# GpSimd's first expert subtractions cut in halves and tied to the routing rounds' comparisons; sixteen filler matmuls a round in place of fifteen

## The chip, the core and the metric

The kernel runs on one core of one Trainium2 chip. Its engines work in parallel, each through a queue of its own: TensorE (PE in the profile, PEld for its weight loads), VectorE (DVE), ScalarE (ACT), GpSimd (POOL) and SyncE (SP), which only issues DMAs here. The metric is the device time of one execution in microseconds, lower is better.

## The reference, cut to what matters

Attention with a decay, a gated FFN, and a routed layer of eight experts follow each other:

```python
attn_out = _attn_ref(**attn_kwargs)                      # 4 x 8 heads, 576 tokens, 64
x = attn_out.transpose(0, 2, 1, 3).reshape(B * S, H * D)  # 2304 x 512
gate = 1.0 / (1.0 + np.exp(-(x @ w_gate)))
x = gate * (x @ w_val) @ w_out
logits = x @ w_gate2                                     # 2304 tokens, 8 experts
for idx in np.argsort(-logits.flatten()):                # best pairs first
    tok, e = divmod(idx, 8)
    if assigned[tok] < 0 and counts[e] < 288:
        assigned[tok] = e
        counts[e] += 1
for e in range(8):
    out[assigned == e] = np.maximum(x[assigned == e] @ w1[e], 0.0) @ w2[e]
```

## The kernel before

Float32 products are made of three matmuls: each operand is split into a high part (a rounded copy, made by ScalarE) and a low part (the operand less the copy, made by GpSimd or VectorE), and high-high, low-high and high-low are summed.

The program runs through attention, FFN, routing and experts. Routing is the place of the change. It needs the logits of all tokens; the FFN's last output matmuls (tokens of the last rows, 7 passes of 36 matmuls, L666, `Ffn.defer`) are kept back and handed out one at a time by `filler(n)`, so that TensorE has work while VectorE does the routing. Each pass ends with an eviction by ScalarE (L669) and a store of x2d by SyncE (L513). After the routing, `filler(1000)` runs what is left; then the experts start with a gather of their tokens from x2d by the indices `idx` (L979, on GpSimd's queue).

Routing is a search by rounds (`ROUNDS = 7`, numbered 0 to 6 here). In a round VectorE

- removes what fell below the last bounds (L786 reads the bounds in PSUM and the logits in SBUF; L787 reads two tiles in SBUF), chooses each token's best expert (L789, L791),
- subtracts the expert's bound (L798, L800, L802) and compares with 64 thresholds: L803, the long comparison, writes the tile `c` (shown as mr),

then TensorE counts in 18 small matmuls (L806) and gets `FILL[4] = 2` fillers, VectorE makes the next step from the counts (L809), TensorE adds it to the bounds in PSUM (L779) and gets `FILL[5] = 15` fillers (6 in the last round). All engines work in the order in which the program is written (a manual schedule), with a wait where one needs what another makes.

Beside this the first expert's first four weight blocks are made ready (`Experts`, blocks 0 to 3, each 128x1024): loaded by SyncE into one of two buffers `fraw`, copied to `ehi` by ScalarE (L956), subtracted to `elo` by GpSimd (L958). Before, `split(r)` stands behind each of rounds 0 to 3, with nothing that ties it to VectorE's place in the round; block n + 2 is loaded when block n is through. The other 60 blocks are split in the expert stage.

Of the kernel before, what the change touches and what calls it, by code (L numbers as in the profile page):

```python
# [6 lines left out]
F32 = mybir.dt.float32  # L7
F32R = mybir.dt.float32r
# [4 lines left out]
AF = mybir.ActivationFunctionType  # L13
OP = mybir.AluOpType
# [10 lines left out]
E = 8  # L25
# [335 lines left out]
class Weights:  # L361
# [5 lines left out]
    def __init__(self, ev, stage, w64):  # L367
        self.ev, self.stage, self.w64 = ev, stage, w64
        self.more, self.ahead = None, 2
        self.hi, self.lo, self.raw, self.b = [None] * NF, [None] * NF, {}, {}  # L370
# [43 lines left out]
class XLoader:  # L414
# [34 lines left out]
    def split(self, c, k, nk=1, steps=(0, 1, 2)):  # L449
        nc = self.ev.nc  # L450
        xh, xl = self.hi[c][:, k:k + nk], self.lo[c][:, k:k + nk]
        x = self.r[c, k]
        for step in steps:
            if step == 0:
                nc.vector.tensor_tensor(x, xl.bitcast(F32), x, op=OP.mult)
            elif step == 1:
                nc.scalar.activation(xh, x, AF.Copy)
            else:
                nc.gpsimd.tensor_tensor(xl, x, xh, op=OP.subtract)
                del self.r[c, k]  # L460


class Ffn:
# [180 lines left out]
    def logits(self, buf, fill):  # L644
# [4 lines left out]
        nc.vector.tensor_copy(s[:, TC:], self.lg[1][:16, :256])  # L649
        fill(FILL[0])  # L650
        p = self.bank()
# [21 lines left out]


TH = 64
FILL = (3, 5, 12, 10, 2, 15, 13, 18)
ROUNDS = 7
MORE = 24

# [22 lines left out]
class Route:  # L702
# [35 lines left out]
    def start(self, L):  # L738
# [6 lines left out]
        nc.vector.tensor_copy(self.Lm, L)  # L745
        self.fill(FILL[1])
        p = self.psum()
# [9 lines left out]
        nc.vector.tensor_scalar(up, s[:E], -1.0, None, op0=OP.mult)  # L757
        self.fill(FILL[2])
        self.lo = self.psum("o0")
        self.raise_by(up, True)  # L760
        self.fill(FILL[3])

# [28 lines left out]
        nc.vector.tensor_tensor(a, self.Lm, self.bcast_t(m), op=OP.is_equal)  # L791
        return a, m

    def round(self, first=False, fill=FILL[5]):
        nc, wk = self.nc, self.work
        a, m = self.choose(first)
        la = self.la
        nc.vector.tensor_tensor(la, a, self.bcast_e(self.lo[:, :E]), op=OP.mult)  # L798
        lt = wk.tile([128, NT], F32, name="r_lt")
        nc.vector.tensor_reduce(lt, la.rearrange("p e t -> p t e"), op=OP.add, axis=AX.X)  # L800
        u = wk.tile([128, NT], BF16, name="r_u")
        nc.vector.tensor_tensor(u, m, lt, op=OP.subtract)  # L802
        nc.vector.tensor_tensor(self.c, self.pairs(u, TH), self.row(self.gs), op=OP.is_ge)  # L803
        cnt = self.psum()
        for t in range(NT):
            nc.tensor.matmul(cnt[:E, :TH], a[:, :, t], self.c[:, t // 2, :, t % 2], start=t == 0, stop=t == NT - 1)  # L806
        self.fill(FILL[4])
        up = wk.tile([E, 1], F32, name="r_up", bufs=2)
        nc.vector.scalar_tensor_tensor(self.g, cnt[:E, :TH], CAP - 0.5, self.ds, op0=OP.is_ge, op1=OP.mult, accum_out=up)  # L809
        self.raise_by(up)  # L810
        self.fill(fill)
# [114 lines left out]
class Experts:  # L926
# [4 lines left out]
    def __init__(self, ev, first, w1, w2):  # L931
        self.ev, self.first, self.pool, self.w1, self.w2 = ev, first, None, w1, w2
        self.raw, self.hi, self.lo = {}, {}, {}

    def load(self, n, queue=None):
        queue = queue or self.ev.nc.sync
# [10 lines left out]
                queue.dma_start(r.rearrange("p (k d) -> p k d", k=2),  # L947
                                          self.w2[e, i * 256:(i + 1) * 256, :].rearrange("(k p) d -> p k d", p=128))

    def split(self, n):  # L950
        if n < 8 * E:
            nc, r = self.ev.nc, self.raw.pop(n)
            pool = self.first if n % 12 < 4 else self.pool
            hi = self.hi[n] = pool.tile([128, 1024], F32R, name=f"ehi{n % 12}", bufs=1)
            lo = self.lo[n] = pool.tile([128, 1024], F32R, name=f"elo{n % 12}", bufs=1)
            nc.scalar.activation(hi, r, AF.Copy)  # L956
            eng = nc.vector if n % 4 == 3 and n > 3 else nc.gpsimd
            eng.tensor_tensor(lo, r, hi, op=OP.subtract)  # L958
            if n < 2:
                self.load(n + 2)  # L960
            elif n > 3:
                self.load(n + RAWS)


RAWS = 4
# [122 lines left out]
def network(tc, qk, vv, f, ww, bcT, w1, w2, cb, cf, out):  # L1088
    nc = tc.nc
    ev = Env()  # L1090
    ev.nc, ev.tc = nc, tc
    with ExitStack() as ctx:
        ctx.enter_context(tc.manual_schedule())

        def pool(name, stack=ctx, side="left", bufs=1, **kw):
            return stack.enter_context(tc.tile_pool(name=name, bufs=bufs, side=side, reuse_waits="tile", **kw))

        ev.consts = pool("consts")
        dr = ctx.enter_context(tc.tile_pool(name="dram", bufs=1, space=bass.MemoryType.DRAM))
        xs = dr.tile([NHEAD, D + 1, S], F32, name="xs")  # L1100
        rec = dr.tile([NHEAD, S], F32, name="rec")
        ckd = dr.tile([2, NHEAD, S], F32, name="ckd")
        x2d = dr.tile([N, DM], F32, name="x2d")
        L = ev.consts.tile([128, E, NT], F32, name="L")
        ev.idx = ev.consts.tile([TT, 24], I32, name="idx")

        body, right = ExitStack(), ExitStack()
        xp = pool("xp", right, "right")
        w0, mix = pool("w0", body), pool("mix", body)
        W = Weights(ev, mix, ww)  # L1110
        W.tiles(w0, 0, -(-EARLY // 3))
        X = XLoader(ev, xp, xs, rec)
        xa = X.tiles(xp, "xa")
        X.put(0, xa)
        X.put(2, xa)
        X.put(4, xa)

        def fill(h):
            if h == -3:
                W.load(0)  # L1120
                W.load(1)
            elif h == -2:
                for step in range(3):
                    W.bits(0, step)
            elif h == -1:
                W.cut(0)
            count = lambda h: 3 + (h - 3) * (EARLY - 1) * 3 // 27
            jobs = lambda h: range(count(h), count(h + 1))
            for lag, do in enumerate((W.bits, lambda n, s: s == 2 and W.cut(n, (0,)),
                                      lambda n, s: s == 2 and W.cut(n, (1,)))):  # L1130
                if 3 <= h - lag < 30:
                    for i in jobs(h - lag):
                        do(*divmod(i, 3))
            if XF <= h < XF + 16:
                k, i = divmod(h - XF, 4)
                if i == 0:
                    X.load(0, k)
                else:
                    X.split(0, k, steps=(i - 1,))

        attention(ev, qk, vv, f, xs, rec, ckd, fill)

        W.tiles(pool("w1", body), -(-EARLY // 3), NF)
        work, ps = ExitStack(), ExitStack()
        xq = pool("xq", right, "right")
        W.more, W.ahead = xq, 4
        xb = X.tiles(xq, "xb")
        X.put(1, xb)
        X.put(3, xb)
        F = Ffn(ev, W, X, EARLY, bcT, x2d, L, pool("pg", ps, bufs=4, space=PSUM), pool("po", ps, space=PSUM))  # L1150
        F.wk, F.mix, F.right = pool("fw", work), mix, xq
        F.wp = F.wk.tile([128, NF, E], F32, name="wp")
        F.wpr = F.wk.tile([128, NF, 2 * E], F32R, name="wpr")
        F.regular()
        F.group()
        right.close()
        work.close()

        ep = pool("ep", side="right")
        tail = ExitStack()  # L1160
        rp, rw = pool("rp", tail), pool("rw", tail, bufs=2)
        scratch = [mix.tile([128, n], F32, name=m, bufs=1) for m, n in (("mr0", 1024), ("mr1", 1024), ("mb0", 512), ("mb1", 512))]
        xd, scratch[0] = scratch[0][:, :DM], scratch[0][:, DM:]
        EW = Experts(ev, ep, w1, w2)
        rest = F.defer(xd)

        def filler(n):
            for _ in range(n):
                if next(rest, 0) == 0:
                    break  # L1170

        R = Route(ev, rp, rw, F.bank, cb, cf, scratch, filler)
        EW.load(0)
        EW.load(1)
        F.logits(scratch[1], filler)
        R.start(L)
        for r in range(ROUNDS):
            R.round(r == 0, FILL[5] if r < ROUNDS - 1 else 6)
            if r < 4:
                EW.split(r)  # L1180
        a = R.settle()
        R.permutation(a)
        filler(1000)
        tail.close()
        body.close()
        ps.close()
        EW.pool = pool("ew")
        xw = pool("xw", bufs=2)
        pools = {n: pool("xp_" + n, bufs=b, space=PSUM) for n, b in (("h", 3), ("y", 2), ("t", 3))}
        experts(ev, EW, x2d, ev.idx, out, xw, lambda n: pools[n].tile([128, 512], F32, name="e" + n))  # L1190
# [30 lines left out]
```

## Time and profile before

| what | value |
|---|---|
| time, median of 3 runs | 943.69 us (939.49, 943.69, 945.07) |
| the profiled execution | 940.77 us, its span 939.1 us |
| granted TensorE clock, mean | 0.978 |
| busy: TensorE | 913.0 us, 97% of the span |
| busy: VectorE | 552.4 us, 59% |
| busy: GpSimd | 454.8 us, 48% |
| busy: ScalarE | 331.0 us, 35% |

All times within the execution count from the start of the span. Busy time of TensorE is pipelined matmuls, so that 97% busy does not mean 97% at full rate. A granted clock of 1.00 is 2.4 GHz, of 0.5 is 1.2 GHz; between the two stands a stretch that had both. A row of a timeline gives start, duration, engine, line, operation, output<-inputs with shapes, and in brackets how long the engine had stood idle and who ended that.

### The profile page before, as it was taken

To read this page: it belongs to the slowest core of one execution; us is meant where nothing else is said; L and a number is where in the kernel's file an instruction comes from. 1 tells how busy PE (TensorE), PEld (TensorE's weight loads), DVE (VectorE), ACT (ScalarE), POOL (GpSimd) and SP (SyncE) were. 2 spreads that over 40 slices of the span, in tenths; PEclk is the share of its full clock that TensorE was granted. 3 is DMA by queue.
4 is the path that set the end of the run, shared out by engine and by line. 5 is a ranking of instruction groups with operands and counts; after the bars stand their busy time and mean duration, and the time that the engine had idled before them with its cause. 6 is when DMAs were issued, how large, how long until landed. Compare 5 with 4: busy or idle time off the path is not lost. (4 is left out here: it accounts for less than half of the span.)

```text
span 939.1 us, 14062 instructions
## 1 busy us (share of the span) xinstructions
PE 913.0 (97%) x5188; PEld 767.1 (82%) x5188; DVE 552.4 (59%) x1188; ACT 331.0 (35%) x570; POOL 454.8 (48%) x376
## 2 busy tenths in 40 slices
PE   8899999999999999999999999998989999999996
PEld 4677777778788888888888888876779999999995
DVE  6467867737886387988989533536504434434431
ACT  4466667643232211121111222121016444444430
POOL 5678879843665122221222222124027787777741
PEclk7799999999999999999999999999899999999998
DMA  5687899754552202010111210012028666665610
GB/s 129 160 215 209 211 220 240 197 157 150 174 162 80 73 0 90 18 63 11 56 51 26 65 45 1 1 55 68 24 66 268 216 190 182 199 187 193 201 48 26
DMA packets 48873, 111.04 MB, mean 118 GB/s; under 512 B 11331, under 2 KB 11747, under 8 KB 48803
## 3 DMA queue, kind: packets, MB, share of 16 engines
q1 hardware_dynamic: 44642, 98.59, 36.6%
q0 software_dynamic: 3072, 9.44, 3.1%
q10 hardware_dynamic: 1088, 2.10, 0.7%
q8 instruction: 41, 0.67, 0.3%
q14 instruction: 30, 0.24, 0.1%
HBM read 86.12 MB, written 14.45 MB: 107 GB/s over the span
## 5 line engine op out<-in xcount | busy, mean ns | idle before, releaser
L497 POOL TENSOR_TENSOR gl<-sg,gh 128x512 fp32r<-128x512 f32 x36 | 50.0, 1388 | 200.9 <-ACT gh L496 200.9
L958 POOL TENSOR_TENSOR elo<-eraw,ehi 128x1024 fp32r<-128x1024 f32 x45 | 108.3, 2416 | 42.0 <-ACT ehi L956 41.6
L145 PE MATMUL pv<-e,vf 128*65 128x256 f32 (+1 forms) x434 | 106.3, 370 | 0.0
L490 PE MATMUL gv<-xah,w_hi 128*128 128x512 f32 (+1 forms) x288 | 103.2, 358 | 0.0
L490 PE MATMUL gv<-xal,w_hi 128*128 128x512 f32 (+1 forms) x288 | 102.9, 357 | 0.0
L490 PE MATMUL gv<-xah,w_lo 128*128 128x512 f32 (+1 forms) x288 | 102.8, 357 | 0.0
L530 DVE CUSTOM_DVE_ANT_0 mb<-mb,bc 128x512 f32<-128x512 f32 x96 | 82.2, 856 | 3.3
L530 DVE CUSTOM_DVE_ANT_0 mb<-mr,bc 128x512 f32<-128x512 f32 x96 | 82.4, 858 | 2.8
L1003 PE MATMUL eh<-xeh,ehi 128*128 128x288 f32 x256 | 78.3, 306 | 0.9 <-DVE hl L1006 0.9
L1016 PE MATMUL ey<-hh,ehi 128*128 128x288 f32 x256 | 78.0, 305 | 0.0
L496 ACT ACTIVATE gh<-sg 128x512 fp32r<-128x512 f32 x36 | 22.8, 633 | 156.5 <-PE o L509 84.3
L1003 PE MATMUL eh<-xel,ehi 128*128 128x288 f32 x256 | 76.7, 299 | 0.0
L1003 PE MATMUL eh<-xeh,elo 128*128 128x288 f32 x256 | 76.4, 299 | 0.0
L1016 PE MATMUL ey<-hl,ehi 128*128 128x288 f32 x256 | 76.4, 299 | 0.0
L490 PE MATMUL gv<-xbh,w_hi 128*128 128x512 f32 x192 | 76.1, 396 | 0.0
L490 PE MATMUL gv<-xbl,w_hi 128*128 128x512 f32 x192 | 76.1, 396 | 0.0
L490 PE MATMUL gv<-xbh,w_lo 128*128 128x512 f32 x192 | 76.0, 396 | 0.0
L1016 PE MATMUL ey<-hh,elo 128*128 128x288 f32 x256 | 75.7, 296 | 0.0
L169 DVE CUSTOM_DVE_ANT_0 mj<-p1b,mq 128x192 bf16<-128x192 f32 (+3 forms) x128 | 46.8, 419 | 45.6 <-PE p1b L145 45.6
L145 PE MATMUL p1b<-P 66*128 66x192 f32 (+7 forms) x256 | 69.3, 339 | 3.4 <-DVE mx L169 2.0
L145 PEld LDWEIGHTS pv<-e,vf 128*65 128x65 f32 x434 | 50.5, 139 | 24.1 <-issue 15.5
L1006 DVE SCALAR_TENSOR_TENSOR hl<-eh,hh 128x288 fp32r<-128x288 f32 x64 | 29.1, 456 | 61.5 <-ACT hh L1005 61.5
(202 smaller groups left out, 2289.1 us busy)
## 6 DMA issues: line engine op xcount, KB each, us to landing
eraw<-w SPq DMA_DIRECT2D x56, 512.0 KB
mr<-ww SPq DMA_DIRECT2D x26, 512.0 KB
raw<-qk SPq DMA_DIRECT2D x16, 576.0 KB
p<-P SPq DMA_DIRECT2D x64, 144.0 KB
vf<-vv SPq DMA_DIRECT2D x16, 330.0 KB
bc<-ww SPq DMA_DIRECT2D x10, 512.0 KB
xs<-xo SPq DMA_DIRECT2D x16, 292.5 KB
xr<-rec SPq DMA_DIRECT2D x32, 128.0 KB
```

The source lines that it names most:

```text
L145: nc.tensor.matmul(out, lhsT, rhs, start=start, stop=stop, skip_group_check=True)
L169: nc.vector.tensor_tensor_reduce(out=junk[:, JT[t]:JT[t] + n], in0=src, in1=ev.mq[:, S - n:], op0=OP.add, op1=OP.min, scale=-1.0, scalar=3 ...
L490: nc.tensor.matmul(p[i][:, :m], w_[:, ws], x_[:, k], start=n == 0, stop=n == 11)
L496: nc.scalar.activation(hi, s, AF.Copy)
L497: nc.gpsimd.tensor_tensor(lo, s, hi, op=OP.subtract)
L530: nc.vector.tensor_tensor_reduce(out=junk, in0=a, in1=self.bc[j], op0=OP.mult, op1=OP.add, scale=1.0, scalar=0.0, accum_out=res)
L958: eng.tensor_tensor(lo, r, hi, op=OP.subtract)
L1003: nc.tensor.matmul(p[:, :CH], w_[:, ws], x_[:, k], start=n == 0, stop=n == 11)
L1006: nc.vector.scalar_tensor_tensor(h[1][:, f], p[:, :CH], 0.0, h[0][:, f], op0=OP.max, op1=OP.subtract)
L1016: nc.tensor.matmul(p[:, :CH], w_[:, ws], h_[:, f], start=n == 0, stop=n == 23)
```

## The change

Blocks 0 to 2 are split in halves: in round r (1 to 6), right behind L803, half (r - 1) % 2 of block (r - 1) // 2. Ahead of each half GpSimd copies one element of `c` to a tile `gate`, which makes it wait for that round's L803. Block 3 follows in two halves behind `idx`. The whole block is still copied to ehi in one piece, with the first half. The next load is issued with the second half. And `FILL[5]` goes from 15 to 16.

```diff
-FILL = (3, 5, 12, 10, 2, 15, 13, 18)
+FILL = (3, 5, 12, 10, 2, 16, 13, 18)
...
-    def round(self, first=False, fill=FILL[5]):
+    def round(self, first=False, fill=FILL[5], beside=lambda: None):
...
         nc.vector.tensor_tensor(self.c, self.pairs(u, TH), self.row(self.gs), op=OP.is_ge)
+        beside()
         cnt = self.psum()
...
+        self.gate = first.tile([1, 1], F32, name="gate", bufs=1)
...
-    def split(self, n):
-        if n < 8 * E:
+    def split(self, n, part=None, after=None):
+
+        if part is not None:
+            nc, c = self.ev.nc, slice(512 * part, 512 * part + 512)
+            if part == 0:
+                self.hi[n] = self.first.tile([128, 1024], F32R, name=f"ehi{n % 12}", bufs=1)
+                self.lo[n] = self.first.tile([128, 1024], F32R, name=f"elo{n % 12}", bufs=1)
+                nc.scalar.activation(self.hi[n], self.raw[n], AF.Copy)
+            nc.gpsimd.tensor_copy(self.gate, after)
+            nc.gpsimd.tensor_tensor(self.lo[n][:, c], self.raw[n][:, c], self.hi[n][:, c], op=OP.subtract)
+            if part:
+                del self.raw[n]
+                if n < 2:
+                    self.load(n + 2)
+        elif n < 8 * E:
...
-            if n < 2:
-                self.load(n + 2)
-            elif n > 3:
-                self.load(n + RAWS)
+            self.load(n + RAWS)
...
         for r in range(ROUNDS):
-            R.round(r == 0, FILL[5] if r < ROUNDS - 1 else 6)
-            if r < 4:
-                EW.split(r)
+            R.round(r == 0, FILL[5] if r < ROUNDS - 1 else 6, lambda: r and EW.split((r - 1) // 2, (r - 1) % 2, R.c[:1, 0, :1, 0]))
         a = R.settle()
         R.permutation(a)
+        for part in range(2):
+            EW.split(3, part, ev.idx[:1, :1])
         filler(1000)
```

GpSimd's queue in the routing rounds, as a piece of the difference (- before, + after; mr_5456 is the tile c, and in brackets stand the semaphores waited for):

```order
 L497 TENSOR_TENSOR w_lo_2236<-mb_5398,w_hi_2235 128x256 [waits Activation_49]
-L958 TENSOR_TENSOR elo_5584<-fraw,ehi_5583 128x1024 [waits DMAHW1_49,DMAHW6_49,Activation_49,Pool_49]
-L958 TENSOR_TENSOR elo_5641<-fraw,ehi_5640 128x1024 [waits DMAHW2_49,PE_49,DMAHW7_49,Activation_49,Pool_49]
-L958 TENSOR_TENSOR elo_5702<-fraw,ehi_5701 128x1024 [waits DMAHW2_49,Activation_49]
-L958 TENSOR_TENSOR elo_5757<-fraw,ehi_5756 128x1024 [waits DMAHW3_49,Activation_49]
-L848 TENSOR_LOAD r_n [waits DVE_49]
-L850 COMPARE_AND_BRANCH
+L960 CAST gate<-mr_5456 1x1 [waits DVE_49,Activation_49,Pool_49]
+L961 TENSOR_TENSOR elo_5598<-fraw,ehi_5597 128x512 [waits DMAHW6_49,DMAHW1_49,Activation_49]
+L960 CAST gate<-mr_5456 1x1 [waits DVE_49]
+L961 TENSOR_TENSOR elo_5598<-fraw,ehi_5597 128x512
```

Before, four whole subtractions stand there that wait for ScalarE and the loads; after, each half has a gate that waits for VectorE in front of it (two more pairs of gates and halves follow, for blocks 1 and 2).

GpSimd's queue behind the routing, in the changed kernel (idx is the list of slots; L991 is the first expert's gather, L979 before):

```order
L851 UNCONDITIONAL_BRANCH [waits Pool_sequencer_49]
L960 CAST gate<-idx 1x1 [waits DVE_49,Pool_49]
L961 TENSOR_TENSOR elo_6140<-fraw,ehi_6139 128x512 [waits DMAHW5_49,Activation_49]
L960 CAST gate<-idx 1x1 [waits Pool_49]
L961 TENSOR_TENSOR elo_6140<-fraw,ehi_6139 128x512
L991 DMA xg<-x2d,idx 96x512 [waits DMAHW4_49,DMAHW3_49,DMAHW6_49,DMAHW1_49,DMAHW7_49,DMAHW0_49,PE_49]
```

Block 3 stands between the branch and the gathers now; before, the gathers followed the branch directly.

SyncE's queue in the rounds, as a piece of the difference (fraw<-w are the loads of blocks 2 and 3, x2d<-mr the stores of finished output rows):

```order
-L944 DMA fraw<-w 128x1024 [waits DMAHW6_49,DMAHW2_49,Pool_49]
-L944 DMA fraw<-w 128x1024 [waits DMAHW7_49,DMAHW3_49,Pool_49]
-L513 DMA x2d<-mr_5455 64x512 [waits DMAHW4_49,Activation_49]
-L513 DMA x2d<-mr_5455 64x512 [waits DMAHW5_49]
+L946 DMA fraw<-w 128x1024 [waits DMAHW2_49,DMAHW6_49,Activation_49,Pool_49]
+L513 DMA x2d<-mr_5455 64x512 [waits DMAHW3_49,Activation_49]
+L513 DMA x2d<-mr_5455 64x512 [waits DMAHW4_49]
+L946 DMA fraw<-w 128x1024 [waits DMAHW5_49,DMAHW7_49,Activation_49,Pool_49]
```

The load of block 3 has moved behind the second pair of stores.

## Rows read from the trace of the kernel before

**Rows 1.** Chain of waits, 610 to 712 us: start, duration, what.

```profile
680.50 10.78 PE o L666 x81
```

**Rows 2.** TensorE's waits in the span: us in total, times, longest.

```profile
PE gv L806 <- DVE mr L803: 3.7, 2, 1.9
```

**Rows 3.** Windows, L806 to L806: length; PE, PEld, DVE, ACT, POOL busy; clock; DMA.

```profile
630.17:635.44 5.27, 5.27 (x39) 3.91 (x38) 3.21 (x10) 2.41 (x3) 0.73 (x1) 1.00 0.10 24
635.44:642.51 7.07, 5.33 (x39) 3.91 (x38) 5.27 (x10) 0.08 (x1) 4.29 (x2) 1.00 0.56 162
642.51:647.77 5.26, 5.26 (x37) 3.91 (x38) 3.20 (x10) 1.90 (x3) 0.28 (x1) 1.00 0.05 18
647.77:655.02 7.25, 5.33 (x39) 4.00 (x39) 5.45 (x10) 0.59 (x1) 4.46 (x2) 1.00 0.14 33
655.02:663.28 8.26, 8.26 (x38) 6.04 (x37) 3.18 (x10) 0.60 (x1) 0.00 (x0) 0.59 0.06 21
```

**Rows 4.** VectorE's timeline, 634 to 681 us.

```profile
634.37 0.76 DVE L803 TENSOR_TENSOR mr<-r_u,r_cb 128x1152 bf16<-128x1152 bf16 x1
...
637.16 0.30 DVE L786 TENSOR_TENSOR mr<-r_lm,o 128x144 f32<-128x144 f32 x1 [0.76 <-PE o L779]
637.50 2.40 DVE L787 SCALAR_TENSOR_TENSOR r_lm<-mr,r_lm 128x144 f32<-128x144 f32 x1
...
641.70 0.76 DVE L803 TENSOR_TENSOR mr<-r_u,r_cb 128x1152 bf16<-128x1152 bf16 x1
...
644.57 0.31 DVE L787 SCALAR_TENSOR_TENSOR r_lm<-mr,r_lm 128x144 f32<-128x144 f32 x1
...
646.70 0.76 DVE L803 TENSOR_TENSOR mr<-r_u,r_cb 128x1152 bf16<-128x1152 bf16 x1
...
649.83 2.57 DVE L787 SCALAR_TENSOR_TENSOR r_lm<-mr,r_lm 128x144 f32<-128x144 f32 x1
...
680.75 0.18 DVE L922 SCALAR_TENSOR_TENSOR idx<-gv,r_pr 96x24 int32<-96x24 f32 x1
```

**Rows 5.** GpSimd's timeline, 630 to 700 us.

```profile
634.71 5.02 POOL L958 TENSOR_TENSOR elo<-fraw,ehi 128x1024 fp32r<-128x1024 f32 x2 [13.98 <-ACT ehi L956]
647.49 4.74 POOL L958 TENSOR_TENSOR elo<-fraw,ehi 128x1024 fp32r<-128x1024 f32 x2 [7.76 <-ACT ehi L956]
695.75 1.11 POOL L979 DMA_INDIRECT xg<-x2d,idx  x1 [43.52 <-issue]
697.16 0.92 POOL L979 DMA_INDIRECT xg<-x2d,idx  x1 [0.31 <-issue]
```

**Rows 6.** TensorE's timeline, 640 to 659 us.

```profile
640.15 0.39 PE L666 MATMUL o<-w_lo,w_hi 128*128 128x512 f32 x1
640.38 0.39 PE L666 MATMUL o<-w_hi 128*128 128x512 f32 x1
642.51 0.71 PE L806 MATMUL gv<-mr,r_a 128*8 128x64 bf16 x18 [1.74 <-DVE mr L803]
...
655.02 0.90 PE L806 MATMUL gv<-mr,r_a 128*8 128x64 bf16 x18 [1.92 <-DVE mr L803]
...
658.54 0.63 PE L666 MATMUL o<-w_hi 128*128 128x512 f32 x1
658.97 0.63 PE L666 MATMUL o<-w_hi,w_lo 128*128 128x512 f32 x1
```

**Rows 7.** GpSimd's groups by line and shape: count, busy us, mean ns, idle before.

```profile
L411 POOL TENSOR_TENSOR w_lo<-mb,w_hi 128x512 fp32r<-128x512 f32 x36 | 53.8, 1503 | 5.1 <-ACT w_hi L408 5.1
...
L203 POOL TENSOR_SCALAR_AFFINE_SELECT e<-e 128x256 f32<-128x256 f32 x32 | 13.9, 434 | 2.2
...
L497 POOL TENSOR_TENSOR w_lo<-gh,w_hi 128x512 fp32r<-128x512 f32 x4 | 5.2, 1292 | 20.8 <-ACT w_hi L496 20.8
...
L1034 POOL MEMSET gap<- 1x1 f32 x24 | 2.1, 88 | 0.0
```

**Rows 8.** ScalarE's timeline, the first two copies to ehi.

```profile
633.52 2.00 ACT L956 ACTIVATE ehi<-fraw 128x1024 fp32r<-128x1024 f32 x2
```

## The prediction, made before the changed kernel was run

> **What bounds the kernel now.** I read the chain of waits first. Between the FFN and the experts it runs along TensorE's fillers, the deferred output matmuls of L666: 81 of them fill the last 10.78 us [rows 1]; behind them come the last store of x2d and the first gather. The number of fillers is fixed, so this stretch ends when TensorE has done them all, and every microsecond in which TensorE stands still or runs slow between them moves the rest of the program. The list of waits then says where it stands still: twice, 3.7 us in all, for the comparison of thresholds L803 [rows 2]. The table of windows, cut from one counting (L806) to the next, puts a price on it [rows 3]. Undisturbed rounds take 5.27 and 5.26 us (the round after the last window shown takes 5.26 too). Three rounds are longer: 7.07, 7.25 and 8.26 us, the last at a granted clock of 0.59 where the others have 1.00.
>
> VectorE's timeline shows why [rows 4]. L787, 128x144 with both operands in SBUF, takes 0.31 us in a quiet round and 2.40 and 2.57 us in two. GpSimd's timeline has two pairs of 128x1024 subtractions, 634.71 to 639.73 and 647.49 to 652.23 [rows 5], and L787 ends 0.17 us after the pair each time (639.90 and 652.40). L786, which reads PSUM and SBUF, runs inside the first pair at its usual 0.30 us [rows 4]. So an SBUF-and-SBUF instruction of VectorE is held until GpSimd is through. TensorE has run out of fillers by then and idles 1.74 and 1.92 us before L806 [rows 6]. After the second idle its matmuls come every 0.43 us (658.54, 658.97) where they came every 0.23 us (640.15, 640.38): the lower of the two levels, 1.2 GHz, for most of one round.
>
> **The change part by part.**
>
> *Whole subtractions leave the rounds' critical places.* What they cost now: 7.07 - 5.26 = 1.81 us, 7.25 - 5.26 = 1.99 us, and 8.26 - 5.26 = 3.00 us for the slow-clock round behind the second idle [rows 3]. The first two agree with the other side of the account: L787 is late by 2.09 and 2.26 us, of which 0.26 us was slack (below), so 1.83 and 2.00 us. If L787 is never held, all three go: **-6.80 us**.
>
> *Six halves come in, in rounds 1 to 6, each behind its round's L803.* The question is whether a half is over when the next L787 starts. From the end of L803 to the next L787 there are 637.50 - 635.13 = 2.37 us, again 649.83 - 647.46 = 2.37 us, and 644.57 - 642.46 = 2.11 us in the round in which TensorE had been waiting [rows 4]. Into this must go: a handoff from VectorE, the gate, a handoff, the half. The trace has no 1x1 copy on GpSimd; below it lies the 1x1 memset, 88 ns, above it the 128x256 select, 434 ns [rows 7]. A 128x512 subtraction takes 1.29 us alone and 1.50 us on average beside a busy VectorE [rows 7]. A handoff takes 0.05 us (L803 ends at 642.46, L806 starts at 642.51 [rows 4, 6]), at most the 0.31 us that GpSimd leaves between two gathers [rows 5]. Low end: 0.05 + 0.09 + 0.05 + 1.29 = 1.48 us. High end: 0.31 + 0.43 + 0.31 + 1.50 = 2.55 us. I take about 1.6 us, near the low end, because a 1x1 copy is nearest to the memset and VectorE is mostly waiting for the counts at this time. That is over 0.5 us ahead of L787. At the high end L787 would be 0.18 to 0.44 us late, which the next part covers. Cost taken: 0.
>
> *The sixteenth filler.* VectorE's own loop, from L806 to the next L806, is 642.51 to 647.46 plus 0.05 = 5.00 us [rows 4, 6], against TensorE's 5.26 us with fifteen fillers. So TensorE sets the round already, with 0.26 us to spare. One more filler is 0.23 us: the round becomes 5.49 us, the slack 0.49 us. The six fillers are taken from the tail, which gets shorter by the same 6 x 0.23 = 1.38 us. Net 0. idx comes 1.38 us later against the fillers, and hides behind the tail: idx is there at 680.93, the gather starts at 695.75 [rows 4, 5].
>
> *The fourth subtraction moves behind idx.* Two gates and two halves, 2 x 1.48 to 2 x 2.55 = 3.0 to 5.1 us, stand ahead of the gathers on GpSimd's queue. Between idx and the gather there are 14.8 us now; with 1.38 us gone from it some 13 us remain. Hidden; if that cover were gone, it would cost its 3.0 to 5.1 us one for one.
>
> *The other queues.* ScalarE's copies to ehi now come one at a time, in rounds 1, 3 and 5, and the last one after the settling. Two took 2.00 us from 633.52 on [rows 8], so the first ends at about 634.5, and its gate opens at 635.13: the half does not wait for it. On SyncE the loads of the third and fourth expert block are no longer together ahead of the second x2d store: one stands before it, one behind, each waiting for a second half. Each store waits for an eviction that comes once in 36 fillers (8.3 us); a load that is released 1.6 us after a comparison holds it up by less than a round, and the two PSUM banks in turn hide that. L803 also waits, as the order of the changed kernel shows, until the gate of the round before has read its tile; that gate is done some 5 us earlier. All 0.
>
> **Sum.** 940.77 - 6.80 = 933.97 us against the profiled execution's own time (its span is 939.10, 1.67 us lie around it). The median of the runs before stands 2.92 us above that execution. Is this offset kept? It is nearly the price of one slow-clock round, 3.00 us. In the profiled execution the first idle was not followed by a slow round, the second was [rows 3]; where both are, the offset belongs to what the change takes away, and the new median is 933.9 us. If it comes from elsewhere, the new median is 943.69 - 6.80 = 936.89 us. I take the middle, **935.4 us**, 0.9% under the median before.
>
> The Trainium skill ("TensorE: Matmul & The Clock Gate", Part 1) says that the unit which gates the clock runs freely and does not start with the kernel, so that the place of a transition shifts. By that rule the same idle may or may not cost a slow round in another execution; taken alone it would speak for 933.9 us. The one profiled execution here shows one idle of each kind and cannot decide it.
>
> **The rivals.**
>
> *More goes than the profiled execution shows* (chance 0.20). Both idles are followed by a slow round in the typical run: 1.81 + 1.99 + 2 x 3.00 = 9.80 us, from 943.69 to 933.9 us. For it: the 2.92 us. Against it: the fastest run before, 939.49 us, is only 1.28 us under the profiled one, which fits no whole round, so other things vary too.
>
> *Half of it stays* (0.15). TensorE still meets a short idle or two in the rounds because gate and half come near 2.55 us or a load comes late, and one slow-clock round of 3.00 us is the result; or the experts' first block gets less out of an earlier start. 935.4 + 3.00 = 938.4 us, up to 941.
>
> *No half is gated* (0.05), because the comparison is long done when GpSimd comes to it (a late ehi or raw block): the holds of L787 return in another place. 941 to 945 us.
>
> *Slower: every half meets L787* (0.05). The place is the start of L787 in six rounds instead of two; the price is the rest of the half, at most 1.29 us, so that VectorE's loop is 5.00 + 1.29 = 6.29 us against 5.49: 0.80 us of idle in each of six rounds, 4.8 us. An idle round followed by a slow one, which covers the next hold, makes three slow rounds, 9.0 us. 940.77 - 6.80 + 4.8 + 9.0 = 947.8 us, and 950.7 with the offset. It decides from the point at which handoffs, gate and half take over 2.37 + 0.49 = 2.86 us; my high end is 2.55.
>
> The Trainium skill ("SBUF — State Buffer", Who interferes with whom) says that whichever of the two engines starts first keeps the ports they share for its whole instruction. By that rule a half that starts late costs its full rest, as I priced it. The trace agrees as far as it goes: L787 ended 0.17 us after the pair that held it [rows 4, 5]. The same page gives the release a lag of about 115 ns, measured with another pair of operations; no row here shows it apart. An estimate from that page's figure: 6 x 0.115 = 0.7 us more for this rival, nothing for the forecast.
>
> **How the numbers follow.** Forecast 0.55, with a range of its own from 932.7 (939.49 - 6.80) to 938.3 (945.07 - 6.80). The rivals take the other 0.45 as given. The range of 932 to 940 leaves out the slower case, the ungated case and the upper end of the half case, about 2 in 10. A measurement of this kernel can tell about 1% from no change, here 9.4 us: faster than 934.25 us. A fifth of the forecast (0.11) and most of the larger gain (0.15) lie there: 0.26. Slower than 953.1 us lies only the far end of the slow rival: 0.02. The rest is the same.
>
> **What would show it.** In the changed kernel's profile L787 takes 0.31 us in all its seven places; GpSimd has six subtractions of about 1.3 us, each starting some 0.2 us after L803 and ending before L787; no wait of L806 for L803 over 0.1 us is in the list; the rounds last 5.49 us at a clock of 1.00; and from the first round's counting to the last filler there are about 6.8 us less than now. I am wrong if a gate takes more than 0.9 us, if the rounds stay uneven, or if the stretch shrinks by 6.8 us and the experts behind it do not start earlier by as much.

## The result, and the profile after

The changed kernel takes 935.03 us, the median of four runs (933.05 to 935.73), against 944.3 us before (939.49 to 945.07, four runs with the last one added): ratio 0.9909, 95% interval 0.9883 to 0.9934. Forecast were 935.4 us and a range of 932 to 940. The profiled execution took 935.39 us, with a span of 933.4.

In the changed kernel L803 keeps its line, the counting is L807, the step L810, the gate L960, the half L961 and the warm-up matmuls behind the fillers L1056 (L806, L809, L958 and L1044 before). The windows of [rows 3], from one counting to the next, over the six gated rounds (length; busy PE, PEld, DVE, ACT, POOL; granted clock; DMA):

```profile
631.24:636.73 5.49, 5.49 (x40) 4.10 (x39) 3.21 (x10) 1.55 (x2) 0.38 (x2) 1.00 0.14 32
636.73:642.21 5.48, 5.48 (x39) 4.10 (x38) 3.20 (x10) 0.00 (x0) 1.44 (x3) 1.00 0.08 18
642.21:647.70 5.49, 5.49 (x39) 4.10 (x39) 3.21 (x10) 1.54 (x2) 1.40 (x3) 1.00 0.49 130
647.70:653.19 5.49, 5.49 (x40) 4.11 (x39) 3.21 (x10) 0.00 (x0) 1.45 (x3) 1.00 0.06 13
653.19:658.67 5.48, 5.48 (x39) 4.09 (x38) 3.22 (x10) 1.55 (x2) 1.38 (x3) 1.00 0.43 145
658.67:664.16 5.49, 5.49 (x39) 4.10 (x39) 3.20 (x10) 0.00 (x0) 1.43 (x3) 1.00 0.01 3
```

All rounds take 5.49 us at the full clock, TensorE is busy through each, and the wait of [rows 2] is gone from the list. VectorE's timeline in the first of these rounds, beside [rows 4]:

```profile
635.43 0.76 DVE L803 TENSOR_TENSOR mr<-r_u,r_cb 128x1152 bf16<-128x1152 bf16 x1
...
638.78 0.31 DVE L787 SCALAR_TENSOR_TENSOR r_lm<-mr,r_lm 128x144 f32<-128x144 f32 x1
```

and GpSimd's from there on, beside [rows 5]:

```profile
636.35 0.18 POOL L960 CAST gate<-mr 1x1 f32<-1x1 bf16 x1 [14.57 <-DVE mr L803]
636.50 1.26 POOL L961 TENSOR_TENSOR elo<-fraw,ehi 128x512 fp32r<-128x512 f32 x1
...
678.23 1.28 POOL L961 TENSOR_TENSOR elo<-fraw,ehi 128x512 fp32r<-128x512 f32 x1
690.04 1.13 POOL L991 DMA_INDIRECT xg<-x2d,idx  x1 [10.53 <-issue]
```

The gate starts 0.16 us after L803 (which ends at 636.19), the half is over at 637.76, 1.57 us after it, and L787 follows at 638.78. The seven L787 take 307 to 309 ns:

```profile
L787 DVE SCALAR_TENSOR_TENSOR r_lm<-mr,r_lm x7: 307/308/309, 633.3 to 666.2; 128x144 f32<-128x144 f32 x7
```

The other five gates are ended by L803 in the same way, and their halves end 1.46 to 1.51 us after it. Block 3 ends at 679.51, 10.5 us ahead of the gather.

The ends of the routing stretch, first filler and first warm-up matmul, from TensorE's timeline:

```profile
621.96 0.40 PE L666 MATMUL o<-w_hi 128*128 128x512 f32 x1
...
685.40 0.62 PE L1056 MATMUL eh<-ehi 128*128 128x512 f32 x2
```

The stretch takes 685.40 - 621.96 = 63.44 us. Before it ran from 620.90 to 691.10, 70.20 us. So it became 6.76 us shorter; the span only 5.7 us, because in this execution everything ahead of the stretch (attention and FFN, which the change does not touch) took 1.06 us longer. What lies behind the stretch takes 248.0 us in both, so all that the stretch lost comes through to the end.

### The profile page after: what moved, and what is told of

It reads as the page before. It is cut to its first block, busy times and chain, and to the rows that moved or that the text cites. A ratio compares the mean times of both kernels' runs of the same rounds, so it can differ in the third digit from the quotient of the medians.

```text
span 933.4 us, 14077 instructions
## 1 busy us (share of the span) xinstructions
PE 911.9 (98%) x5187; PEld 767.1 (82%) x5188; DVE 550.2 (59%) x1188; ACT 330.7 (35%) x570; POOL 456.3 (49%) x388
## 5 line engine op out<-in xcount | busy, mean ns | idle before, releaser
L145 PE MATMUL pv<-e,vf 128*65 128x256 f32 (+1 forms) x434 | 108.6, 376 | 0.0
```

The source lines that it names most:

```text
L145: nc.tensor.matmul(out, lhsT, rhs, start=start, stop=stop, skip_group_check=True)
```

## The experiments

The stretch is the sharper measure here, since what lies ahead of it differs by some us between executions, while what lies behind it took 247.2 to 248.8 us in all thirteen profiles. Each stretch is that of one profiled execution. Ratios are to the kernel before, measured beside each group of runs: e1 to e4 form one group, a1 and e5 to e7 another, all on one chip; b1 to b3 are single executions on another chip and have no ratio. The last column is the longest L787.

| run | stretch, us | ratio to before (95%) | L787, us |
|---|---|---|---|
| before | 70.20 | 1 | 2.57 |
| changed kernel | 63.44 | 0.9909 (0.9883 to 0.9934) | 0.31 |
| e1, sixteen fillers alone | 66.11 | 0.9969 (0.9950 to 0.9987) | 2.17 |
| e2, the halves with fifteen | 63.40 | 0.9947 (0.9927 to 0.9966) | 0.31 |
| e3, no gate | 64.04 | 0.9950 (0.9931 to 0.9969) | 0.31 |
| e4, before with twenty-four fillers | 68.61 | 1.0003 (0.9984 to 1.0021) | 2.29 |
| a1, the changed kernel again | 63.41 | 0.9911 (0.9882 to 0.9940) | 0.31 |
| e5, whole blocks behind L803 | 63.41 | 0.9913 (0.9881 to 0.9945) | 0.31 |
| e6, whole blocks behind the step | 66.25 | 0.9949 (0.9921 to 0.9977) | 1.77 |
| e7, the halves on VectorE | 63.45 | 0.9896 (0.9859 to 0.9932) | 0.31 |
| b1, b2, b3, before again | 70.21, 70.19, 69.83 | | 2.57, 2.57, 2.39 |

A stretch that is 6.8 us shorter makes a ratio of 0.993 by itself. What the stretches give in this way lies inside the interval of every run but e4, where it is 0.9983 against an interval that begins at 0.9984.

**Sixteen fillers alone.**

```diff
-FILL = (3, 5, 12, 10, 2, 15, 13, 18)
+FILL = (3, 5, 12, 10, 2, 16, 13, 18)
```

> The kernel before with sixteen fillers a round and whole, untied subtractions. My theory (VectorE's L787 is held by GpSimd's pair of subtractions, TensorE runs out of fillers, and the clock falls after it): one filler covers 0.23 us of each hold, so the two idles shrink to about 1.5 and 1.7 us and a slow-clock round stays; the gain is about 0.5 us of the 6.8, ratio to before 0.999 to 1.000 (up to 0.996 if the slow round is missed by chance). Rival, the filler theory (the sixteenth filler is what gives VectorE its slack): most of the gain, ratio about 0.991, and L787 not over 0.5 us.

VectorE in the first held round, and the windows of the third to sixth round:

```profile
642.39 2.17 DVE L787 SCALAR_TENSOR_TENSOR r_lm<-mr,r_lm 128x144 f32<-128x144 f32 x1
```

```profile
640.33:647.18 6.85, 5.56 (x40) 4.10 (x39) 5.05 (x10) 0.00 (x0) 4.06 (x2) 1.00 0.55 157
647.18:652.66 5.48, 5.48 (x38) 4.09 (x38) 3.21 (x10) 2.49 (x3) 0.95 (x1) 1.00 0.18 47
652.66:659.51 6.85, 5.56 (x40) 4.19 (x39) 5.05 (x10) 0.00 (x0) 4.07 (x2) 1.00 0.05 13
659.51:664.98 5.47, 5.47 (x39) 4.08 (x38) 3.19 (x10) 0.60 (x1) 0.00 (x0) 1.00 0.12 48
```

L787 still takes 2.17 us and two rounds are long, each by 6.85 - 5.49 = 1.36 us; 1.29 us of it is the idle (expected 1.5 and 1.7), but no slow-clock round follows. The stretch, 66.11 us, is 2.7 us over the changed kernel's, which is the two long rounds; the other 4.1 us of the gain were there with the filler alone, 3.0 of them the slow-clock round and 1.1 the shorter idles. The ratio, -0.3% with an interval from -0.1 to -0.5%, agrees with 4.1 us and is over the 0.5 us that I had expected in the usual case. So in this profile the sixteenth filler's worth was mostly in the clock, not in its 0.23 us a round; that it keeps the clock in every execution is not shown. By the stretch the filler alone gives most of the gain, as the filler theory has it, though not its ratio of 0.991; its mechanism is wrong: L787 takes over 0.5 us, and the next run has the whole gain without the filler.

**The halves with fifteen fillers.** The changed kernel with `FILL[5] = 15`.

> The changed kernel with fifteen fillers. My theory: halves end before L787, VectorE's loop of 5.00 us is still inside TensorE's 5.26, no idle, no slow round; the same time as the changed kernel within 0.5 us, ratio to before about 0.991. Filler theory: back to the time before, ratio near 1.00, with waits of L806 for L803 in the list.

One of its windows:

```profile
643.19:648.45 5.26, 5.26 (x39) 3.91 (x38) 3.21 (x10) 1.55 (x2) 1.40 (x3) 1.00 0.37 107
```

Rounds of 5.26 us throughout, L787 never held, stretch 63.40 us. The sixteenth filler adds nothing to the stretch once the holds are gone. The ratio, 0.9947, is not the 0.991 that I expected; the run of the changed kernel below comes back to that.

**No gate.**

```diff
-            nc.gpsimd.tensor_copy(self.gate, after)
```

> The changed kernel without the copies to gate: GpSimd takes a half as soon as ehi is there, and the second half right behind it, one block every second round. My theory asks only whether a subtraction stands across L787's start: ehi of each block is done at about the end of L803's run (635.6, 646.7, 657.6), two halves then end 2.5 to 3 us later, just before or at L787's start: L787 late by at most 0.3 us, covered by the slack, ratio to before about 0.991. Rival, the gate theory (a half must be tied to the comparison, or it meets the round's two-tile instructions): L803 or L787 held over 1 us in three rounds, idles of 0.5 to 1 us and at least one slow-clock round, ratio 0.995 to 1.00.

GpSimd's first pair of halves and that of block 3, and the L787 behind the first:

```profile
641.24 2.78 POOL L960 TENSOR_TENSOR elo<-fraw,ehi 128x512 fp32r<-128x512 f32 x2 [13.98 <-ACT ehi L959]
...
676.15 2.60 POOL L960 TENSOR_TENSOR elo<-fraw,ehi 128x512 fp32r<-128x512 f32 x2 [10.17 <-ACT ehi L959]
```

```profile
644.26 0.31 DVE L787 SCALAR_TENSOR_TENSOR r_lm<-mr,r_lm 128x144 f32<-128x144 f32 x1
```

In the rounds L787 is never held; the first pair of halves ends at 644.02, and L787 comes at 644.26. Nothing ties the pair to that place: it started when ScalarE's copy behind an eviction ended, at 641.10, and in this program that is close to L803's end, 641.65. The stretch is 0.6 us longer, and VectorE's timeline shows where: block 3, no longer tied to idx, runs from 676.15 to 678.75, into the making of the permutation.

```profile
676.63 0.95 DVE L903 TENSOR_TENSOR mr<-mr,r_af 128x144 f32<-128x144 f32 x1
...
678.07 0.71 DVE L907 TENSOR_SCALAR r_st<-r_st 128x18 f32<-128x18 f32 x1
```

The changed kernel has 0.31 and 0.17 us there. TensorE waits 0.4 us for the last comparison (L915) then. The gate theory fails for the rounds in this program and holds for block 3. Its ratio, 0.995 to 1.00, came all the same: 0.9950, where I expected 0.991.

**Twenty-four fillers, whole blocks.** The kernel before with `FILL[5] = 24`.

> The kernel before with twenty-four fillers a round and whole, untied subtractions. L787 is held as before (2.4 and 2.6 us), but TensorE has 5.26 + 9 x 0.23 = 7.3 us of work in a round, over the 7.25 us that a held round took. My theory (the price of the hold is TensorE's idle time and the clock behind it, nothing else): no wait of L806 for L803 over 0.2 us, no slow round, the same time as the changed kernel, ratio to before about 0.991. Rival (the hold delays the routing itself, and the experts wait for idx): the end of routing comes 9 x 6 x 0.23 = 12.4 us later against the fillers, idx reaches the gather late, and the ratio is 0.996 or above.

The ratio is 1.000 and not 0.991. The fillers shifted the evictions and with them ScalarE's copies, so blocks 0 and 1 did not meet L787; blocks 2 and 3 came as a pair into one round. VectorE there, and the windows of that round and the next:

```profile
657.35 2.29 DVE L787 SCALAR_TENSOR_TENSOR r_lm<-mr,r_lm 128x144 f32<-128x144 f32 x1
...
660.12 1.95 DVE L791 TENSOR_TENSOR r_a<-r_lm,r_m 128x144 bf16<-128x144 f32 x1
```

```profile
655.29:663.89 8.60, 7.37 (x48) 5.69 (x47) 6.80 (x10) 2.49 (x3) 4.83 (x2) 1.00 0.08 31
663.89:672.76 8.87, 8.87 (x47) 6.72 (x46) 3.18 (x10) 0.60 (x1) 0.00 (x0) 0.81 0.09 31
```

The first subtraction held L787, the second L791: 3.6 us in one round, where an undisturbed one of 7.30 us covers 2.3 us over VectorE's loop of 5.00. The round is 1.30 us longer (1.23 us of it idle), and 1.57 us of slow clock follow. So whether a hold inside the cover is free was not tested here; the price of one beyond it came out. At the end of the stretch TensorE waits 1.24 us for the permutation:

```profile
686.92 0.28 PE L666 MATMUL o<-w_hi,w_lo 128*128 128x256 f32 x1
687.04 0.28 PE L666 MATMUL o<-w_lo,w_hi 128*128 128x256 f32 x1
688.57 0.99 PE L917 MATMUL gv<-mb,mr 128*96 128x48 bf16 x18 [1.24 <-DVE mr L914]
```

The 18 fillers ahead of it are the narrow ones of the last passes, one every 0.12 us, since the rounds have used up the wide ones (0.23 us). For the same reason 0.60 us go ahead of L820 and 0.4 us more than before at the branch (L850). With 1.30 and 1.57 us that makes 5.1 of the 5.20 us over a1. The rival's ratio came, its reason did not: idx was written at 689.99, and the gather started 7.2 us later. Covering a hold with TensorE's work takes that work from the tail.

**The changed kernel again.**

> The changed kernel once more, beside the three that follow and on the same chip. The stretch from the first filler (L666) to the warm-up matmuls (L1044) was 70.20 us before and 63.44 us in the changed kernel, 63.40 with fifteen fillers and 64.04 without gates. My theory: again 63.4 us, and a ratio to before like that of the fifteen-filler kernel on its chip (0.993 to 0.997), since neither the sixteenth filler nor the gate adds anything. Rival, the two parts do add something (the first measurement, 0.9909, against 0.9947 and 0.9950 without one of them): ratio 0.992 or lower here too.

Stretch 63.41 us, ratio 0.9911: the first result repeats. The ratio is the rival's (0.992 or lower) and not mine (0.993 to 0.997); the stretch is mine. e2 and e3 stood 3.5 us above a1 by ratio, measured beside other runs of the kernel before, with stretches 0.01 us under and 0.63 us over a1's; their intervals overlap a1's. The stretch decides for my theory on the filler; the ratios alone would not have. The medians here, 936.75 and 943.08 us, are 6.3 us apart.

**Whole blocks behind the comparison.** In the changed kernel:

```diff
-            nc, c = self.ev.nc, slice(512 * part, 512 * part + 512)
+            nc, c = self.ev.nc, slice(0, 1024)
...
-            nc.gpsimd.tensor_copy(self.gate, after)
-            nc.gpsimd.tensor_tensor(self.lo[n][:, c], self.raw[n][:, c], self.hi[n][:, c], op=OP.subtract)
-            if part:
+                nc.gpsimd.tensor_copy(self.gate, after)
+                nc.gpsimd.tensor_tensor(self.lo[n][:, c], self.raw[n][:, c], self.hi[n][:, c], op=OP.subtract)
+            if part == 0:
```

> The changed kernel with whole blocks: one 128x1024 subtraction behind the comparison of rounds 1, 3 and 5. My theory: gate at 0.16 us after L803, the subtraction from 0.3 to 2.7 us after it, L787 due 2.6 us after it: L787 late by 0.1 to 0.3 us in three rounds, inside the 0.49 us of slack; stretch 63.4 to 63.7 us, the same ratio as the changed kernel within 0.001. Rival, the halving is needed: L787 late by over 0.5 us, idle time of L806, stretch 64.5 us or more.

GpSimd and VectorE in its first such round:

```profile
637.62 2.36 POOL L961 TENSOR_TENSOR elo<-fraw,ehi 128x1024 fp32r<-128x1024 f32 x1
```

```profile
639.91 0.31 DVE L787 SCALAR_TENSOR_TENSOR r_lm<-mr,r_lm 128x144 f32<-128x144 f32 x1
```

The subtraction ends at 639.98, 0.07 us into L787 (0.11 and 0.03 us in the other two rounds), and L787 is neither late nor longer. Stretch 63.41 us: the halving is not needed.

**Whole blocks behind the step.** As e5, with the gate on the step made from the counts (the edit below is against e5):

```diff
-        beside()
...
+        self.up = up
+        beside()
         self.raise_by(up)
...
-            R.round(r == 0, FILL[5] if r < ROUNDS - 1 else 6, lambda: r and EW.split((r - 1) // 2, (r - 1) % 2, R.c[:1, 0, :1, 0]))
+            R.round(r == 0, FILL[5] if r < ROUNDS - 1 else 6, lambda: r and EW.split((r - 1) // 2, (r - 1) % 2, R.up[:1, :1]))
```

> The same whole blocks, but each gated on the step made from the counts (L810's r_up) in place of the comparison, so that it starts about 0.8 us ahead of L787. This is the slow rival of the prediction, made to happen in three rounds. My theory: L787 late by about 1.5 us in each, less 0.49 us of slack: an idle of about 1.0 us before L806 in three rounds, and a slow-clock round of up to 3.0 us behind some of them; stretch 66.3 us without a slow round, up to 75 with three; ratio 0.003 to 0.012 above the changed kernel's. Rival, the hold is not what costs (what counts is that subtractions are one block at a time): stretch 63.4 us.

GpSimd, VectorE and TensorE in its first such round:

```profile
637.09 2.39 POOL L962 TENSOR_TENSOR elo<-fraw,ehi 128x1024 fp32r<-128x1024 f32 x1
```

```profile
637.88 1.75 DVE L787 SCALAR_TENSOR_TENSOR r_lm<-mr,r_lm 128x144 f32<-128x144 f32 x1
```

```profile
642.28 0.71 PE L806 MATMUL gv<-mr,r_a 128*8 128x64 bf16 x18 [0.90 <-DVE mr L803]
```

The same number of the same subtractions, one at a time, only 1.5 us later in the round: L787 ends 0.15 us after GpSimd, 1.44 us later than it would alone, and the round is 6.46 us, 0.97 over 5.49 (1.44 - 0.49 = 0.95). Three such rounds make 2.86 us, and the stretch is 2.84 us longer than a1's, with no slow clock. Between e5 and e6 only the place in the round differs (copy, subtraction and load move together), so this is the hold, its slack and its price in one. It also fits e5: a held L787 ends 0.15 to 0.17 us after GpSimd and a free one 0.31 us after its own start, so that an overlap of up to some 0.15 us, an estimate from these rows, should cost nothing.

**The halves on VectorE.** In the changed kernel:

```diff
-            nc.gpsimd.tensor_copy(self.gate, after)
-            nc.gpsimd.tensor_tensor(self.lo[n][:, c], self.raw[n][:, c], self.hi[n][:, c], op=OP.subtract)
+            nc.vector.tensor_tensor(self.lo[n][:, c], self.raw[n][:, c], self.hi[n][:, c], op=OP.subtract)
```

> The changed kernel with the halves on VectorE, right behind the comparison, and no gate. VectorE idles there for 1.2 us until the counts come, and a 128x512 subtraction takes about 0.6 us on it (a 128x1024 one 1.23). My theory: with GpSimd out of the rounds there is nobody to hold L787, the halves fit the idle time, stretch 63.4 us, the same ratio as the changed kernel within 0.001. Rival, VectorE's loop becomes the bound (5.00 us plus 0.6 is over 5.49): rounds of 5.6 us, stretch 64.1 us.

VectorE in its first such round:

```profile
637.87 0.68 DVE L960 TENSOR_TENSOR elo<-fraw,ehi 128x512 fp32r<-128x512 f32 x1
639.24 0.21 DVE L810 SCALAR_TENSOR_TENSOR mr<-gv,r_ds 8x64 f32<-8x64 f32 x1 [0.68 <-PE gv L807]
```

A half takes 0.68 us out of VectorE's wait for the counts and leaves 0.68 us of it. Stretch 63.45 us, all rounds 5.49: the same as on GpSimd, without a gate. Its ratio cannot be told from the changed kernel's.

**The kernel before, three times more.**

> The kernel before, unchanged, for its profile: is the slow-clock round part of every execution? The prediction left open whether the 2.92 us between the profiled execution and the median go with the change. If the clock rounds vary: the stretch from the first filler to L1044 is 67.2 us with no slow round, 70.2 with one, 73.2 with two, and its idles are 1.8 and 2.0 us each time. If they do not vary, 70.2 us here too, and the offset comes from outside the stretch (the start of attention, whose end lay between 620.9 and 627.4 us in the profiles so far).

> The same again: 67.2, 70.2 or 73.2 us if the clock rounds vary, 70.2 us if not.

> The same again: 67.2, 70.2 or 73.2 us if the clock rounds vary, 70.2 us if not.

The stretch is 70.21, 70.19 and 69.83 us, while the spans are 940.4, 943.1 and 938.0: the offset comes mostly from ahead of the stretch, which begins at 622.32, 624.95 and 620.88. What the clock takes is the same in sum, but not always in one piece. b3's rounds:

```profile
635.42:642.49 7.07, 5.34 (x39) 3.92 (x38) 5.27 (x10) 0.08 (x1) 4.29 (x2) 1.00 0.55 162
642.49:649.33 6.84, 6.84 (x37) 5.05 (x37) 3.18 (x10) 2.38 (x3) 0.76 (x1) 0.75 0.10 27
649.33:656.10 6.77, 5.34 (x39) 4.00 (x38) 4.97 (x10) 0.11 (x1) 3.98 (x2) 1.00 0.09 21
656.10:662.91 6.81, 6.81 (x38) 5.04 (x37) 3.18 (x10) 0.60 (x1) 0.00 (x0) 0.75 0.02 8
```

Here both idles were followed by a lower clock, for half a round each: 1.58 + 1.55 = 3.13 us, against 3.00 in the first profile and 3.06 and 3.01 us in b1 and b2, where it was one round.

## Why the prediction was right

- **The holds and the idles.** Right. L787 is held where a subtraction of GpSimd stands across its start by more than e5's 0.11 us (e6 brings that about), and not elsewhere. The sum of the three terms was 6.80 us, and 6.76 (6.79 in a1) went.
- **Halves end before L787.** Right: 1.57 us after L803 where 1.6 were taken. The terms were 0.16 for the first handoff (0.05 taken), 0.18 for the gate (0.09 to 0.43), nothing for the second handoff (0.05; the half starts 0.03 before the gate's record ends), 1.26 for the half (1.29). L787 came 2.59 us after L803 in that round (2.51 to 2.53 in the others) and not 2.37, since the sixteenth filler moves the counts later too.
- **The sixteenth filler costs and brings nothing by itself.** Right with the halves (e2). Alone it was worth 4.1 us in the one profile of it (e1), mostly through the clock, which I had not priced.
- **The queues and block 3.** Nothing of them shows in the stretch, and block 3 ends 10.5 us ahead of the gather. That block 3's place matters was not in the prediction: without its gate it costs 0.6 us (e3).
- **The offset to the median: the wrong step.** I had taken half of 2.92 us, on the thought that it might be a second slow round. Four profiles of the kernel before have a stretch of 69.8 to 70.2 us whatever their span, so most of what sets executions apart lies ahead of the stretch, and no second slow round that the change could remove is in any of them. 936.9 us was the better reckoning, and a1 has 936.75. That the first result, 935.03, came within 0.4 us of the forecast is luck: 6.8 us of 943 are 0.7%, and the rest of its 0.9% is not in the stretch. The rival with 9.8 us falls with this. Of the two in between nothing came: no idle and no slow round is left, and L803 ended the wait of all six gates.
- **The slower rival.** It needed over 2.86 us from L803 to the end of a half; it took 1.57, and a whole block 2.66 (e5). The bound itself was too low, since it put the slack of sixteen fillers on the gap of fifteen: 2.51 to 2.59 us and 0.49 make 3.0 to 3.1. In e6, beyond that point, the mechanism came: about 0.90 us of idle in each of three rounds, which were 2.86 us longer in all, less than the 6.8 us gained. The slow-clock rounds that made the rival slower than before did not come. Nor do the rows show the lag of 0.115 us that the estimate added at the release: a held L787 ended 0.15 to 0.17 us after GpSimd, sooner than 0.115 and its own 0.31 us would have it.
- **The Trainium skill on the clock** ("TensorE: Matmul & The Clock Gate", Part 1): that the place of a transition shifts is borne out by b3. That this would change the sum is not: 3.0 to 3.1 us in all four.

## What to carry to other kernels

When a long instruction of one engine holds up a short one of another, look for the moment at which the short chain does not run into it, and tie the long instruction to the event that opens it; as long as it fitted into the gap, neither its size nor its engine counted here, only its place. A stall that is followed by a lower TensorE clock costs more than its length (1.92 us of idle, 3.00 us more behind it), so its price is read from a window per round and not from idle time. Where the head of a program varies by more than the change is worth, measure the stretch that was changed in several profiles.

## What was not expected of the hardware

A VectorE instruction with one SBUF input was longer beside GpSimd too: L907, a tensor_scalar of 128x18 from SBUF to SBUF, took 0.71 us in e3, up to 0.03 us after the end of block 3, and 0.17 us in the changed kernel. The Trainium skill ("SBUF — State Buffer", Who interferes with whom) counts tensor_scalar among the instructions that can take the shared ports; the row agrees.

```profile
671.96 0.17 DVE L907 TENSOR_SCALAR r_st<-r_st 128x18 f32<-128x18 f32 x1
```

When the clock falls is open. It fell after idles of 1.92 us (before, b1 and b2), 1.73 and 1.43 (b3) and 1.23 (e4), and not after 1.71 to 1.74 (the first idle of before, b1 and b2), two of 1.29 (e1) or three of about 0.90 us (e6). So the length of the idle alone does not decide it. Open too is the spread ahead of the stretch, which began between 620.88 and 627.43 us. TensorE's waits in attention's first heads differ between executions: the one for ScalarE's exponentials was 6.0 us in b2 and 0.2 us in the changed kernel's first profile. They do not make up the spread by themselves: between these two the stretch began only 2.99 us later in b2, whose granted clock over the first 48 us was 0.82 against 0.72. No run was made on it.

```profile
PE p1b L145 <- ACT e L199: 6.0, 1, 6.0
```

```profile
PE p1b L145 <- ACT e L199: 0.2, 1, 0.2
```
